# Linear attention beside a Mish feed-forward, one core: two pairs of token tiles turned when only centred, key weights by transposing loads, and a new order

## The chip, the cores and the metric

The kernel runs on one core of a Trainium2 chip. What counts is the device time of one execution in microseconds (us). The kernel before has a median of 154.43 us in three runs (154.17, 154.43 and 155.7).

The names of the engines in this text: PE does matmuls and transposes (PEld is its load of the stationary operand), ACT activations, DVE vector work, POOL vector and mask work, SP only issues DMAs. ACT can issue DMAs too. "SPq" and "ACTq" in the profile are the instruction queues of the two in which DMA issues show.

## The reference

`x` is 2048 tokens by 448 columns in bfloat16. It is normalised over the columns, and the result is x plus two branches of the normalised `xn`:

```python
def _layernorm(x, axis=-1, eps=1e-5):
    m = jnp.mean(x, axis=axis, keepdims=True)
    v = jnp.var(x, axis=axis, keepdims=True)
    return (x - m) / jnp.sqrt(v + eps)
...
qkv = (x @ wqkv).reshape(B, S, 3, H, Dh)           # H = 16, Dh = 28
pq = jnp.einsum("bhsd,hdf->bhsf", q, w_phi)        # pk likewise from k
phi_q = concatenate([_softmax(pq), _softmax(-pq)]) # phi_k likewise
kv = jnp.einsum("bhsf,bhsd->bhfd", phi_k, v)
z  = jnp.einsum("bhsf->bhf", phi_k)
num = jnp.einsum("bhqf,bhfd->bhqd", phi_q, kv)
den = jnp.einsum("bhqf,bhf->bhq", phi_q, z)[..., None] + 1e-6
o = (num / den) @ wo
...
h = x @ w1 + b1                                    # 448 -> 1792
act = h * jnp.tanh(softplus(h))                    # Mish
ffn = act @ w2                                     # 1792 -> 448
...
return x + A(xn) + B(xn)
```

## The kernel before, in words

**Tiles.** The 2048 tokens are 16 tiles (`t`) of 128, taken as 8 pairs (`u`). A row of 448 columns is three chunks of 128 and one of 64; in the turned pair (`xnT`, 7 chunks of 128 by 128) the two 64s of a pair share one chunk. So each product of a pair has an "F" part (three full chunks for each of its two tiles, six matmuls) and an "H" part (one 64-row matmul for each tile, on the two halves of the array). `pair_part` (L414) issues them in either order; whichever comes second is followed by the evacuation of PSUM. PSUM has 8 banks, used in four pairs of banks; `take2` gives the pair that has been idle longest, in program order.

**Stages.** For each pair: statistics (`ln_stats`, L443), 1/std (`ln_rstd`, L461, on ACT by Ln and Exp or on POOL by a power), normalising (`ln_pair`, L475, on DVE, or on POOL after a small `shift` on DVE), and turning (`xT`, L508, on PE with an evacuation, or by a transposing DMA on SP). Meanwhile the weights of keys and queries are folded with `w_phi`: the key weights are loaded as they stand, turned on PE (`w_tr`, L540) and evacuated to `WT`; the query weights are loaded by four transposing DMAs (`load_qT`, L279), of which a last 64 columns are doubled by a DVE copy (`double_qT`, L283, step `qd`). `w_mm` (L563) multiplies both with a block-diagonal `Wbd` (built on POOL from `w_phi` and a mask) into `Wp`. Then for each pair three products: `v_mm` (values, evacuated by ACT or DVE), `k_mm` and `q_mm` (each evacuated by two ACT exponentials, of the product and its negative). `k_norm` sums the exponentials on DVE and divides on POOL (line L625); `kv_mm` sums over all pairs into one matrix, which `kvz` masks and turns by a DMA. `q_turn` (L680) turns the query exponentials by DMA, tile by tile. `nd` (L708) multiplies them with that matrix on PE and divides on DVE, `oT` turns the outcome by DMA.

The feed-forward (`ffn1`, L691) computes 14 blocks of 128 hidden columns for each half `q` of the tokens, with a Mish on ACT as evacuation. `ffn2` (g, L811) and `wo` (L823) add both branches in one PSUM bank for each tile, `finish` adds x on DVE, `store` writes it.

**The order.** There is no planner at run time. The string ORDER (L147) is a list of step names, and each step appends its instructions to the queues of the engines it uses; each engine executes its own queue strictly in this order. So the string sets the order on PE, ACT, DVE, POOL and of the DMAs on SP all at once, and an instruction that waits holds back what stands behind it on its engine. Names to follow: `lx2s` loads x's tiles 4 and 5 by SP (x4: tiles 8 to 11, x6: 12 to 15), `z12` issues twelve dummy matmuls, `st2b` are the statistics of pair 2 with one tile on DVE and one on ACT, `rs2p` 1/std on POOL, `xn2d` normalising on DVE, `xt2b` turning on PE with the evacuation on ACT and DVE, `xt1m` turning by DMA, `wtk0b` turning half of the key weights, `wmk0b` and `wmq0d` the folding, `v2Fd` the F part of pair 2's values with DVE to evacuate, `kn4.1` the normalising of pair 4's negative exponentials, `e6` the turning of tile 6's query exponentials, `f1.2H` the H part of block 2 for the second half. At the start the two loads of x2 and x3 stand first, then the key weights, `phi`, tails and biases, and x1, v's weights, x4, the query weights, all on SP.

Of the kernel before, what the change touches and what calls it, by code (L numbers as in the profile page):

```python
# [12 lines left out]
D = 448  # L13
H = 16
DH = 28
# [152 lines left out]
def _kernel(es, nc, A_x, A_wqkv, A_w_phi, A_wo, B_w1, B_b1, B_w2, out):  # L168
# [28 lines left out]
    Wkv = sb("Wkv", [P, 4, 2 * D], BF16)  # L197
    Wk, Wv = Wkv[:, :, 0:D], Wkv[:, :, D:2 * D]
# [3 lines left out]
    zeros = sb("zeros", [P, 2], BF16)  # L202
# [9 lines left out]
    WT = [Eq0[0:GP, i * 1024:(i + 1) * 1024].rearrange("p (c g n) -> p c g n", c=2, g=G) for i in range(2)]  # L212
# [753 lines left out]
```

## Time and profile before

| | us |
|---|---|
| median of 3 runs | 154.43 |
| lowest, highest | 154.17, 155.7 |
| span of the profiled execution, first to last instruction | 152.5 |
| first dummy matmul | 0.95 |
| first useful PE instruction | 6.70 |
| first product of x (v2) | 9.87 |
| first exponential on ACT | 14.44 |
| first POOL division of k_norm | 27.88 |
| first kv product | 55.40 |
| last matmuls end, end of span | 149.5, 152.5 |

The profile comes from one execution, whose span from its first to its last instruction is 152.5 us; its own device time is not listed apart from the runs', and the median of the runs is 1.9 us above the span. The page of the profile has six parts: busy time of each engine, the span in 40 slices with a digit for tenths of busy time, DMA queues, the chain of work that ended last, the costliest groups of instructions by line, and DMA issues. Further views list an engine's instructions in order of time (start, duration, engine, line, operation, what is written and read, how many in a row, and in brackets the idle time before with its releaser), who waited for whom, and the instructions of one tile. A matmul's record lasts longer than the distance to the next one, since matmuls are pipelined; so distances of starts are what one reads for PE.

### The profile page before, as it was taken

To read this page: it belongs to the slowest core of one execution; us is meant where nothing else is said; L and a number is where in the kernel's file an instruction comes from. 1 tells how busy PE (TensorE), PEld (TensorE's weight loads), DVE (VectorE), ACT (ScalarE), POOL (GpSimd) and SP (SyncE) were. 2 spreads that over 40 slices of the span, in tenths; PEclk is the share of its full clock that TensorE was granted. 3 is DMA by queue.
4 is the path that set the end of the run, shared out by engine and by line. 5 is a ranking of instruction groups with operands and counts; after the bars stand their busy time and mean duration, and the time that the engine had idled before them with its cause. 6 is when DMAs were issued, how large, how long until landed. Compare 5 with 4: busy or idle time off the path is not lost.

```text
span 152.5 us, 2888 instructions
## 1 busy us (share of the span) xinstructions
PE 147.9 (97%) x1181; PEld 72.7 (48%) x1181; DVE 101.2 (66%) x227; ACT 74.9 (49%) x91; POOL 39.9 (26%) x58
## 2 busy tenths in 40 slices
PE   7899999999998999999999999999999999999993
PEld 2365444454443466444444444555555555455552
DVE  1699997999999203198999847798695970311221
ACT  4888899898599996757459657100000000000000
POOL 7452552499999950000000000000000000000000
PEclk9999999999999999999999999999999999999999
DMA  5995576889969176830379941030206111110302
GB/s 130 274 238 97 175 136 127 177 236 257 189 141 192 24 160 55 135 71 0 64 149 302 338 75 25 4 62 6 54 0 195 50 34 26 60 34 0 120 0 90
DMA packets 39961, 17.17 MB, mean 113 GB/s; under 512 B 33932, under 2 KB 39180, under 8 KB 39948
## 3 DMA queue, kind: packets, MB, share of 16 engines
q1 hardware_dynamic: 39804, 16.89, 49.2%
q8 instruction: 9, 0.15, 0.4%
q10 hardware_dynamic: 144, 0.10, 0.2%
q14 instruction: 4, 0.03, 0.1%
HBM read 7.02 MB, written 1.84 MB: 58 GB/s over the span
## 4 chain that ended last, share of the span: by engine, by line
PE 82%; DMA 7%; ACT 6%; SPq 2%; DVE 0%; issue 0%; ACTq 0%
PE PS L426 40%; PE PS L816 28%; PE PS L832 7%; DMA EqT<-actT 4%; DMA Wkv<-in_A_wqkv_dram 3%; PE PS L716 3%; PE PS L642 2%; ACT actT L613 2%; ACT actT L693 1%; ACT actT L674 1%; PE PS L575 1%; ACT L693 1%; ACT v_all L504 1%; SPq L268 1%; SPq L682 1%; PE PS L551 0%
## 5 line engine op out<-in xcount | busy, mean ns | idle before, releaser
L426 PE MATMUL PS<-xnT,W 128*128 128x512 bf16 (+1 forms) x224 | 46.3, 379 | 0.0
L816 PE MATMUL PS<-W,actT 128*128 128x448 bf16 (+1 forms) x224 | 42.8, 351 | 0.0
L693 ACT ACTIVATE actT<-PS,b1T 128x1024 bf16<-128x1024 f32 x28 | 30.3, 1114 | 13.1 <-PE PS L426 13.0
L816 PEld LDWEIGHTS PS<-W,actT 128*128 128x128 bf16 x224 | 21.8, 98 | 20.2 <-issue 0.4
L426 PEld LDWEIGHTS PS<-xnT,W 128*128 128x128 bf16 (+1 forms) x224 | 17.6, 97 | 23.7 <-issue 5.1
L625 POOL TENSOR_TENSOR actT<-actT,rSk 128x896 bf16<-128x896 bf16 x16 | 26.6, 1701 | 4.4 <-DVE rSk L623 4.4
L781 DVE TENSOR_TENSOR x_all<-PS,x_all 128x448 bf16<-128x448 f32 (+1 forms) x16 | 9.6, 617 | 20.9 <-PE PS L816 17.7
L621 DVE TENSOR_REDUCE Sk<-actT 128x32 f32<-128x896 bf16 x16 | 16.7, 1042 | 0.9 <-ACT actT L613 0.9
L613 ACT ACTIVATE actT<-PS 128x896 bf16<-128x896 f32 x16 | 13.7, 940 | 0.4 <-PE PS L426 0.4
L426 PE MATMUL PS<-Wpq,xnT 128*128 128x448 bf16 (+1 forms) x64 | 12.9, 353 | 0.5 <-ACT actT L693 0.5
L426 PE MATMUL PS<-Wpk,xnT 128*128 128x448 bf16 (+1 forms) x64 | 12.7, 353 | 0.0
L426 PE MATMUL PS<-Wkv,xnT 128*128 128x448 bf16 (+1 forms) x64 | 12.6, 353 | 0.0
L731 DVE COPY Sq<-PS 128x16 f32<-128x16 f32 x32 | 4.0, 167 | 10.8 <-PE PS L716 10.8
L456 DVE BATCH_NORM_STATS2 stats<-x_all 128x6 f32<-128x448 bf16 x14 | 8.5, 605 | 3.4 <-DMA x_all<-in_A_x_dram 3.4
L739 DVE TENSOR_TENSOR v_all<-v_all 128x464 f32<-128x464 f32 x16 | 10.3, 642 | 0.6
L735 DVE TENSOR_TENSOR v_all<-PS,Sq 128x464 f32<-128x464 f32 x16 | 10.3, 641 | 0.5
L742 DVE TENSOR_TENSOR xn<-v_all,rden 128x448 bf16<-128x448 f32 x16 | 10.0, 625 | 0.6
L737 DVE TENSOR_TENSOR v_all<-PS,Sq 128x464 f32<-128x464 f32 x16 | 10.1, 629 | 0.0
L674 ACT ACTIVATE actT<-PS 128x896 bf16<-128x896 f32 x10 | 8.5, 932 | 1.7 <-DMA EqT<-actT 1.7
L426 PEld LDWEIGHTS PS<-Wpq,xnT 128*128 128x128 bf16 (+1 forms) x64 | 5.3, 97 | 6.5 <-issue 1.1
L426 PEld LDWEIGHTS PS<-Wpk,xnT 128*128 128x128 bf16 (+1 forms) x64 | 5.3, 97 | 6.1 <-issue 1.9
L426 PEld LDWEIGHTS PS<-Wkv,xnT 128*128 128x128 bf16 (+1 forms) x64 | 5.0, 97 | 5.7 <-issue 1.5
(86 smaller groups left out, 118.0 us busy)
## 6 DMA issues: line engine op xcount, KB each, us to landing
W<-in_B_w_dram SPq DMA_DIRECT2D x1, 1568.0 KB, 7.8
out_dram<-x_all SPq DMA_DIRECT2D x7, 224.0 KB, 2.2
W<-in_B_w_dram SPq DMA_DIRECT2D x1, 1344.0 KB, 9.0
x_all<-in_A_x_dram SPq DMA_DIRECT2D x4, 224.0 KB, 3.2
x_all<-in_A_x_dram SPq DMA_DIRECT2D x2, 448.0 KB, 4.6
Wkv<-in_A_wqkv_dram SPq DMA_DIRECT2D x2, 336.0 KB, 4.5
Wo<-in_A_wo_dram SPq DMA_DIRECT2D x2, 336.0 KB, 3.9
W<-in_B_w_dram SPq DMA_DIRECT2D x2, 224.0 KB, 3.6
```

Of the source, the lines that this page charges most:

```text
L426: ins = e.matmul(o, lhs(c, k), rhs(c, k), start=first and c in (0, 3), stop=not first and c in (2, 3))
L613: op("ACT", lambda e, s=s: e.activation(E_of(u)[:, s, :, :], two(b, D), ACT.Exp, scale=1.0 if s == 0 else -1.0), r=[pb(b), pb(b + 1)], w=[ ...
L621: op("DVE", lambda e: e.tensor_reduce(Sk[u][:, s, :], Eh(), AX.X, ALU.add), r=[("E", u, s)], w=[("Sk", u, s)], tag=f"Sk{u}.{s}")
L625: op("POOL", lambda e: e.tensor_tensor(Eh(), Eh(), ap_on(rSk[u][:, s, 0:1], [[1, 2 * H], [0, DH]]), ALU.mult), r=[("E", u, s), ("rSk", u, ...
L674: op("ACT", lambda e, s=s: e.activation(Eq_of(u)[:, :, s, :].rearrange("p i (h n) -> p i h n", n=64)[:, :, :, 0:QP], two(b, D).rearrange(" ...
L693: op("ACT", lambda e: e.activation(actT[:, fc, q * 1024:(q + 1) * 1024], bank(b, 2), ACT.Mish, bias=b1T[:, fc:fc + 1]), r=[("b1T",), pb(b) ...
L735: op("DVE", lambda e: e.tensor_tensor(tv(t1[i]), num(0), sx(1), ALU.mult), r=[pb(b), pb(b + 1), ("Sq", i, 1)], w=[("t1", i)], tag=f"ta{t}")
L737: op("DVE", lambda e: e.tensor_tensor(tv(t2), num(1), sx(0), ALU.mult), r=[pb(b), pb(b + 1), ("Sq", i, 0)], w=[("t2",)], tag=f"tb{t}")
L739: op("DVE", lambda e: e.tensor_tensor(t1[i], t1[i], t2, ALU.add), r=[("t1", i), ("t2",)], w=[("t1", i)], tag=f"tc{t}")
L742: op("DVE", lambda e: e.tensor_tensor(o_sb[(t // 2) % 2][:, t % 2, :].rearrange("p (h d) -> p h d", d=DH), t1[i][:, :, 0:DH], ap_on(rden[i ...
L816: ins = e.matmul(bank(b)[:, 0:width(t)], actT[:, fc, tok(t)], W2[:, fc, 0:width(t)], start=first and fc == 0, stop=last and fc == FC - 1)
L832: ins = e.matmul(bank(b)[:, 0:n], oT_of(u)[lo:hi, cc * P:(cc + 1) * P], Wo[lo:hi, cc, 0:n], start=first and c in (0, 3), stop=last and c i ...
```

## The change

- **Two pairs turned when only centred.** For pairs 1 and 3 (`CEN`) a new step `xc` subtracts the mean on DVE without 1/std; `xtc1a` and `xtc3a` turn this on PE into `cT`, which lies in the still unused block 0 of `actT`, with the evacuation on ACT. The value products of these two pairs read `cT`, and their evacuation multiplies by 1/std, tile by tile. Both pairs are normalised in full too (`xn1p`, `xn3p` on POOL) and turned by DMA (`xt1m`, `xt3m`) for everything else. Pair 2 is turned on PE as before; pair 3 no longer in its normalised form.
- **Key weights by four transposing loads.** `w_tr` goes, with its 16 transposes on PE and their evacuations; `load_T` loads the key weights turned, as it does those of the queries, and `kd` doubles their last 64 columns on DVE. Values keep a main load and two tails.
- **Statistics, 1/std and W1 in finer steps.** `ln_stats` takes one tile; W1 is loaded in three chunks and two tails, with its chunks further apart in the order.
- **Dummies.** `z16` instead of `z12`, on the constant 1.0, without a memset to wait for.
- **Order.** A new ORDER. The first DMAs are on two queues: ACT issues x2, x1, v's tails and phi ahead of its table load, x3 right behind it, x4 behind pair 2's evacuation and x0 behind that of centred pair 1; SP issues the first key load, v's main load, the other three key loads, the four query loads, `xt1m`, x6, `xt3m` and so on. Pairs 0, 1, 3, 4 are normalised on POOL, 2, 5, 6, 7 on DVE. PE begins with the dummies, `xt2b`, `xtc1a`, the values of 2 and 1, `wmk`, pair 3's turn, `k2F`, `wmq`, the values of 3.

```diff
 ORDER = """
...
+lx2a lx1a pi z16 pw pv st5d st4d lvta lpa lkT2s lvms table lkT3s lx3a pm rs2a lkT1s st3d lkT0s st2a xn2d xc1 bd rs1p
+xt2b lqT3s lqT2s lx4a xtc1a v2Fa st7d xn1p kd st6d lqT1s lqT0s xc3 rs3p lx0a v2Ha v1Hd wmk0a wmk1b st8d xt1m v1Fa
+xtc3a xn3p qd st10d st9d k2F st11d wmq1a wmq0a st0d lx6s v3Fd rs5a v3Hd pp rs4p xn4p k2H k1H k1F q1F q2H st1d q1H xt3m
+st12d st14d st15d k3H l1ts k3F q2F xn5d rs7p rs0p q3F st13d xt4m rs6p xt5m v4Fd xn7d l1m0s xn0p pk k4H xn6d v4Hd q3H
+k4F kn3.0 kn1.0 lbs xt7m v5Fd xt6m k5F xt0m k5H v5Hd e4 e5 e7 l1m1s e6 k7H v7Hd k7F v7Fa v0Fd k6F kn4.0 kn2.0 kn2.1 b1
+k6H kn4.1 l1m2s q6H v0Hd kn5.1 e3 k0H k0F e2 q6F q4F q5F q5H e12 e13 e11 f0.3H v6Ha ep kn5.0 kn6.1 q4H kn6.0 v6Fd e9
+f0.3F f1.3F e8 f1.0F f1.3H q7H f1.0H kn7.0 kn0.1 kn0.0 kn3.1 q0H q7F q0F f0.0F f0.2F f1.10F f0.0H f0.2H kn7.1 kv3 kv6
+kv2 l2s kv5 e14 kv0 kv4 los kn1.1 kv7 kv1 kvz e15 e1 f1.1H f0.1H f1.10H f0.1F f0.12F f1.1F f1.12F f1.12H f0.12H f1.9H
...
+wo3H nd12 nd13 g7 g8 wo4F wo3F wo2F g4 nd14 nd15 sto4 ot6m g5 wo6F g6 ot7m g14 g10 g11 g12 wo5H wo6H wo7H wo2H wo7F
+wo5F g13 g15 sto2 sto3 sto6 sto1 sto5 sto0 stt14 stt15
...
+    CEN = (1, 3)
+    cT = {u: actT[:, 0, n * 1024:n * 1024 + 7 * P].rearrange("p (c n) -> p c n", n=P) for n, u in enumerate(CEN)}
...
+    def load_T(name, dst, at, g, eng):
+        dma(eng, lambda e: e.dma_start_transpose(dst[:, g, 0:D], A_wqkv[:, at + g * GP:at + g * GP + P]), w=[(name, g)],
+            tag=f"ld{name}{g}")
...
+    def ln_center(u):
+        X = xn[u % NXN]
+        for t in (2 * u, 2 * u + 1):
+            parts = [(0, D, 0)] if t % 2 == 0 else [(384, D, D), (0, 384, D + 64)]
+            for n, (lo, hi, at) in enumerate(parts):
+                op("DVE", lambda e, t=t, lo=lo, hi=hi, at=at: e.tensor_scalar(
+                    X[:, at:at + hi - lo], x_all[:, t, lo:hi], mv[:, t, 0:1], 0.0, op0=ALU.subtract, op1=ALU.add),
+                   r=[("x", t), ("mean", t)], w=[("xn", u % NXN, t % 2, n)], tag=f"xc{t}.{n}")
...
-    def w_tr(h, eng):
...
     def w_mm(which, h, eng):
         b = take2(False)
         n = GP
 
+        name, T = (("WqT", WqT), ("WkT", WkT))[which]
+
         def lhs(c, g):
-            if which:
-                return WT[h][:, c, g, :]
-            return WqT[0:GP, g, (2 * h + c) * P:(2 * h + c + 1) * P]
+            return T[0:GP, g, (2 * h + c) * P:(2 * h + c + 1) * P]
...
     def v_mm(u, part, eng):
         def then(b):
-            evac(eng, lambda: v_all[:, u, :, :, 0:DH], lambda: two(b, D).rearrange("p i (h d) -> p i h d", d=DH),
-                 [pb(b), pb(b + 1)], [("v", u)], f"ve{u}")
...
+            for i in range(2):
+                t = 2 * u + i
+                dst = v_all[:, u, i, :, 0:DH]
+                src = bank(b + i)[:, 0:D].rearrange("p (h d) -> p h d", d=DH)
+                if eng == "ACT":
+                    fn = lambda e, t=t, dst=dst, src=src: e.activation(dst, src, ACT.Copy, scale=rstd[:, t:t + 1])
+                else:
+                    fn = lambda e, t=t, dst=dst, src=src: e.tensor_scalar(dst, src, rstd[:, t:t + 1], 0.0, op0=ALU.mult,
+                                                                          op1=ALU.add)
+                op(eng, fn, r=[pb(b + i), ("rstd", t)], w=[("v", u, i)], tag=f"ve{t}")
```

207 lines of the change are left out of this document (94 added, 113 removed).

## The prediction

> **What bounds the kernel now.** I read the page first, then the chain of waits, then the waits of PE alone, then the timeline of each engine over the first 60 us.
>
> ```profile
> span 152.5 us, 2888 instructions
> ...
> PE   7899999999998999999999999999999999999993
> ...
> ACT  4888899898599996757459657100000000000000
> ```
>
> Only in the last slice is PE below 7 tenths. ACT is nearly as full up to slice 16; at the end it is free. The page warns that ends of matmuls are modelled, so I look at where matmuls start. The chain of waits gives their pace, and its last pieces give the tail:
>
> ```profile
> 7.97 0.65 PE PS L551 x8
> 8.63 0.40 PE PS L499 x7
> ...
> 9.14 0.89 PE PS L575 x16
> ...
> 139.28 10.23 PE PS L816 x56
> ...
> 149.53 0.56 DVE x_all L781
> ```
>
> Transposes go at 0.40/7 = 0.057 us each, the small weight products (L575) at 0.056, the 448-column matmuls at 10.23/56 = 0.183. After the last matmul 152.5 - 149.5 = 3.0 us are left, the last sum and its store. PE's own waits, and the rows at the start and around its one long gap:
>
> ```profile
> PE PS L551 <- DMA Wkv<-in_A_wqkv_dram: 0.7, 2, 0.4
> PE PS L426 <- ACT actT L693: 0.5, 1, 0.5
> ...
> 0.95 5.30 PE L371 MATMUL PS<-zeros 128*128 128x512 bf16 x12 [0.95 <-POOL zeros L314]
> 6.70 0.63 PE L551 MATMUL PS<-ident,Wkv 128*112 128x128 bf16 x8 [0.45 <-DMA Wkv<-in_A_wqkv_dram]
> 7.18 0.56 PE L499 MATMUL PS<-ident,xn 128*128 128x128 bf16 x7
> ...
> 40.01 6.43 PE L426 MATMUL PS<-xnT,W 64*128 64x512 bf16 x32
> 46.90 0.36 PE L426 MATMUL PS<-Wpq,xnT 64*128 64x448 bf16 x2 [0.46 <-ACT actT L693]
> ```
>
> So this execution is 6.7 us of start, 142.8 us of PE that hardly pauses, 3.0 us of tail. Two places lose time after 6.70. The 15 transposes from 6.70 need 15 x 0.057 = 0.86 and would be through at 7.56, but the next start at 7.97: 0.41 lost on the key weights' landing. And the last of the 32 starts at 40.01 + 6.43 - 0.38 = 46.06, the next could follow some 0.3 later, and starts at 46.90: about 0.55 lost on ACT. About 1.0 us can be won there; beyond this only fewer PE steps or an earlier start can help. ACT, DVE and POOL count only where PE waits for them.
>
> **The change part by part, PE's work.** Sixteen transposes of the key weights go (2 x 8, 16 x 0.057 = -0.91); seven of pair 3 come, since pairs 1, 2, 3 instead of 2 and 3 are turned on PE (+0.40). All other products are the same in number and size. The order changes how often PE goes between full-height steps and half-height ones (the 64-row "H" parts, and nd):
>
> ```profile
> 24.50 0.35 PE L426 MATMUL PS<-Wpq,xnT 64*128 64x448 bf16 x2
> 24.69 0.35 PE L426 MATMUL PS<-Wpk,xnT 64*128 64x448 bf16 x2
> 24.97 1.31 PE L426 MATMUL PS<-Wkv,xnT 128*128 128x448 bf16 x6
> ```
>
> Two H parts are 0.19 apart, an H part and the full one behind it 0.28: a change of height costs 0.09. Counted in the two orders, these changes go from 42 to 44: +0.19. Sum of PE's work: -0.91 + 0.40 + 0.19 = **-0.3**.
>
> **The start.** Sixteen dummies instead of twelve, on a constant, so from about 0.75. At 5.30/12 = 0.44 each they end at 7.8. But PE goes at full pace from 6.70 on (the transposes at 0.057), while the dummies go at half of it (512 columns in 0.44, against 448 in 0.183 later). If the turn comes as early as 6.7 again, 13 are done by then and three go at about 0.22: 7.3. I take 7.3, bounds 7.0 and 7.8. Their input is ready before:
>
> ```profile
> 0.80 0.86 SPq L268 DMA_DIRECT2D x_all<-in_A_x_dram  x2
> 0.80 1.28 ACT L308 ACT_TABLE_LOAD   x1 [0.80 <-PEq L951]
> ...
> 3.39 0.63 DVE L456 BATCH_NORM_STATS2 stats<-x_all 128x6 f32<-128x448 bf16 x1 [3.39 <-DMA x_all<-in_A_x_dram]
> 4.05 0.18 DVE L458 BATCH_NORM_AGGREGATE mv<-stats 128x2 f32<-128x6 f32 x1
> ...
> 11.47 0.89 DVE L491 TENSOR_SCALAR xn<-x_all,mv,rstd 128x448 bf16<-128x448 bf16 x3
> ...
> 7.92 0.48 ACT L504 ACTIVATE xnT<-PS 128x384 bf16<-128x384 bf16 x1
> ...
> 9.16 0.91 ACT L504 ACTIVATE xnT<-PS 128x896 bf16<-128x896 bf16 x1
> ```
>
> x2 is still the first load, now from ACT's queue, so the statistics begin near 3.4, and three tiles take 3 x 0.78: 5.7. ACT issues five DMAs (0.43 each as SP's two, tails and phi somewhat more: 3.4), then the table load (4.7), then one more (5.1), then two small steps for 1/std, about 0.5 together: 5.7. xn2 ends at 6.7, the centring of pair 1 at 7.7. The start is thus **+0.6** against 6.70, set by the dummies and not by data. Then pair 2 is turned, evacuated (0.48 on ACT, DVE beside it) and v2 begins at 8.3; pair 1 is turned beside that. A gap of about **+0.1** is left; 0 to 0.5 are its bounds.
>
> The Trainium skill ("TensorE: Matmul & The Clock Gate", Part 1) says that the array runs at half its clock until a window of about 3.4 us of sustained work has passed, and that this window runs free of the kernel's start. The half pace of the twelve dummies agrees; when it ends was seen here in one execution only. By that rule the dummies would end anywhere from 6.0 to 7.7 (an estimate), and the sum would move by -0.5 to +0.4.
>
> **The first weights.** The key weights now come by four transposing loads on SP, the query ones behind them; most of x and v's tails go out on ACT. The tile view of WqT has, for its four loads,
>
> ```profile
> DMA to landing us min/median/max: 3.0/3.8/4.8
> ```
>
> and of x:
>
> ```profile
> DMA to landing us min/median/max: 2.6/3.8/4.8
> ```
>
> From the timelines of SP, DVE and POOL:
>
> ```profile
> 5.49 0.49 SPq L268 DMA_DIRECT2D x_all<-in_A_x_dram  x1
> 6.02 5.11 SPq L280 DMA_TRANSPOSE WqT<-in_A_wqkv_dram  x4
> ...
> 13.85 0.23 DVE L284 COPY WqT<-WqT 128x256 bf16<-128x256 bf16 x1
> ...
> 15.47 1.14 DVE L506 CAST Wpq<-PS 128x448 bf16<-128x448 f32 x2
> ...
> 17.50 0.15 DVE L479 SCALAR_TENSOR_TENSOR shift<-mv,rstd 128x2 f32<-128x2 f32 x1
> ...
> 17.76 1.74 POOL L486 TENSOR_SCALAR xn<-x_all,rstd,shift 128x448 bf16<-128x448 bf16 x3 [1.11 <-DVE shift L479]
> ```
>
> At 1.28 an issue and 0.43 for v's main load, the fourth key load is issued at 5.1 and lands at 8.1 to 9.9. Its copy (kd) stands on DVE behind tile 7's statistics and pair 1's shift, done at 9.5; PE, after v2 (1.3) and v1's H part, which waits for pair 1's evacuation (ACT, 9.6), gets there at 9.85. No wait; 0.7 if it lands at its latest. PE then has wmk (0.9), v1F (1.1), pair 3's turn (0.4) and k2F (1.1): 13.5. Now it wants the query weights, whose copy (qd) is behind st8 on DVE, and st8 waits for x4, which is issued on ACT's queue behind pair 2's evacuation, at 8.2 instead of 5.49. It lands 3.8 to 4.8 later (median and far end of x's row; it is one of the two large ones): 12.0 to 13.0. st8 0.8, shift 0.15, qd 0.23: 13.2 to 14.2. PE waits **+0.3** (bounds 0 and 0.7). Queued behind qd are st10, st9, st11, st0 (0.78 each), v3's evacuation (2 x 0.6, as the CASTs above) and pair 4's shift.
>
> **Pair 4.** Its xn moves from DVE (0.89) to POOL (1.74). From qd at 13.9: four statistics and v3's evacuation end at 18.2, POOL at 20.0, its transposing load lands 3.0 later at 23.0. PE by then has done wmq and v3 (13.8 + 0.9 + 1.3 = 16.0), and of k2, k1, q1, k3, q2, q3 five F parts, five H parts and some changes of height (5.6 + 1.0 + 0.3): 22.9. **+0.2**, bounds 0 and 0.7.
>
> **ACT, and the old gaps.** ACT gets one turn more (0.91) and the other half of the query weights (about as much), and loses two key evacuations, one tile's statistics and two v evacuations, each of them of the size of these rows or less; so it has no more to do in all. But its first exponentials come behind the evacuations of v2, wmk, v1, pair 3 and wmq, at about 16.9 instead of 14.44 (first row below): from 10.0 on 0.9, 1.5, 1.1, 0.9, 2.0 and 0.5 for pair 5's 1/std. I let the old losses go (**-1.0**) and put **+0.4** for PE waiting on PSUM that ACT has not read, with bounds of 0 and 1.1, twice the 0.55 measured now.
>
> ```profile
> 14.44 1.73 ACT L613 ACTIVATE actT<-PS 128x896 bf16<-128x896 f32 x2
> ...
> 30.32 24.89 POOL L625 TENSOR_TENSOR actT<-actT,rSk 128x896 bf16<-128x896 bf16 x15 [0.74 <-DVE rSk L623]
> ...
> 55.40 3.33 PE L642 MATMUL PS<-actT,v_all 128*60 128x112 bf16 x128
> ```
>
> POOL does three xn more (5.2), all before 26, in time that it idles now; phi then starts near 27.5 and needs 16 x 1.66 = 26.6: 54.1. PE reaches the first kv near 53.5 and the last at 56.4. Cost nothing; if that cover goes, each microsecond of POOL is one of PE.
>
> **Tail.** Same last token, same 3.0. Four stores are now queued behind token 13's sum on SP: **+0.1**, bounds 0 and 0.5.
>
> **Sum.** +0.6 - 0.3 + 0.1 + 0.3 + 0.2 - 1.0 + 0.4 + 0.1 = +0.4 on a span of 152.5. The runs' median, 154.43, stands 1.9 above that span; I add to it: **154.8 us**. With all bounds low the sum is -1.0, with all high +4.0.
>
> **The rivals.**
> A, DVE's queue becomes the bound: x4, 448 KB, shares the DMA engines with the four query loads (112 KB each). Their bytes begin to move near 9.9; 0.9 MB from there, at the 150 to 280 GB/s of these slices
>
> ```profile
> GB/s 130 274 238 97 175 136 127 177 236 257 189 141 192 24 160 55 135 71 0 64 149 302 338 75 25 4 62 6 54 0 195 50 34 26 60 34 0 120 0 90
> ```
>
> take 3.2 to 6 us: landing 13.1 to 15.9, and PE waits 0.8 to 3.5 at qd; all of DVE's later work shifts with it. With the middle (landing 14.5, wait 2.2 instead of 0.3) the time is 156.7. It decides, by 1%, from a landing at about 13.8 on. For it: st8 heads a strict queue. Against: x's row has 4.8 at most, and much was in flight then too. The Trainium skill ("DMA: Bandwidth & Descriptors", "Issuing engines are not separate DMA queues") has the loads of both issuers share the same 16 engines; no run here shows it for ACT and SP together.
> B, no new wait: dummies end at 7.0, the gaps at qd, pair 4 and PSUM are nil: +0.3 - 0.3 - 1.0 + 0.1 = -0.9, 153.5. For it: each of these waits is a few tenths between bounds that include nil. Against: four must be nil together.
> C, the middle: ACT's later start or POOL's phi holds kv back by 1.5 us: 155.9 to 156.3. For it: ACT's slices of 7 to 9 tenths up to slice 16. Against: ACT has less to do in all.
> D, it does nothing: normalising was never what PE waited for, so centred pairs gain nothing, and the order's small changes cancel: 154.4.
>
> **How the numbers follow.** My forecast 0.40 (153.9 to 155.6), D 0.15, A 0.18, C 0.12, B 0.15. About 1% (1.5 us) is what a measurement of this kernel can tell from no change: 152.9 and 156.0 are the borders. B falls below the lower one with an earlier start too, 0.08, and 0.02 come from the edges of the others: faster 0.10. Most of A (0.16), half of C (0.06) and a tenth of my own (0.04): slower 0.26. Same 0.64. Range: the low end takes B with 0.6 to spare (152.9), the high end takes A's middle (156.9).
>
> **What would show it.** First transposes of xn (L499's step) at 7.0 to 7.8; v2's first matmul near 8.3; the query weights' product (L575's second group) near 14.0, with the copy WqT as its releaser and st8 waiting for x_all on DVE; the first kv product at 53 to 55 (now 55.40); the last matmul near 149.9. I am wrong if PE waits over 1 us in one place before 25 us, if ACT's first exponentials come after 18, or if POOL's phi starts after 29.

## The result and the profile after

The changed kernel takes 155.94 us (median of 14 runs, 155.22 to 156.64), the kernel before on the same chip 154.57 (14 runs, 153.7 to 155.7). The ratio is 1.0082, 95% interval 1.0062 to 1.0102: the change costs 1.4 us, slower by 0.8%, which is inside the 1% that the forecast took as no change. The profiled execution of the changed kernel took 155.95 us, with a span of 153.9 against 152.5 before. 1.4 more in the span is the whole difference, so what follows is read from these two spans. Some executions of the variants below lose a few us to a reduced granted clock of PE; the ratios leave out those more than 1.5% above the fastest of their kernel, and the profiled executions of runs 2, 7 and 10 are of this kind (0.989, 0.979 and 0.989 in the mean), so that only their front is read.

The page of the changed kernel, its first line and the slices of PE:

```profile
span 153.9 us, 2901 instructions
...
PE   7779999999999999999999999999999999999992
```

PE is as full as before, from slice 3 to the last but one. No slice shows where 1.4 us went; such small losses only show in the waits of PE and in the distances of its starts. PE's waits by releaser (total, how many, the longest):

```profile
...
PE PS L563 <- DVE WkT L289: 0.8, 1, 0.8
PE PS L563 <- DVE WqT L289: 0.4, 1, 0.4
PE PS L428 <- issue: 0.3, 1, 0.3
```

The wait for pair 2's `xn` before the first turning is left out here. In the changed kernel L507 is the turning of x, L563 the folding of key or query weights, L289 the doubling copy `kd` or `qd`, L428 the products. The old wait for the landing of the key weights is gone; two waits for the doubled weights and one for nothing that the profile names have come. The same places in PE's timeline:

```profile
0.85 4.93 PE L374 MATMUL PS<-const-bfloat16-1.0 128*128 128x512 bf16 x16 [0.85 <-PEq L961]
6.74 1.19 PE L507 MATMUL PS<-ident,xn 128*128 128x128 bf16 x14 [0.96 <-DVE xn L490]
7.88 1.60 PE L428 MATMUL PS<-Wv,xnT 128*128 128x448 bf16 x8
9.32 0.35 PE L428 MATMUL PS<-Wv,actT 64*128 64x448 bf16 x2
10.49 0.96 PE L563 MATMUL PS<-Wbd,WkT 112*128 112x112 bf16 x16 [0.81 <-DVE WkT L289]
...
12.81 1.30 PE L428 MATMUL PS<-Wpk,xnT 128*128 128x448 bf16 x6
14.48 0.96 PE L563 MATMUL PS<-Wbd,WqT 112*128 112x112 bf16 x16 [0.37 <-DVE WqT L289]
...
37.83 2.73 PE L428 MATMUL PS<-Wpq,xnT 128*128 128x448 bf16 x14
40.89 0.39 PE L428 MATMUL PS<-xnT,W 64*128 64x512 bf16 x2 [0.33 <-issue]
```

Read by starts: the first transposes come at 6.74, as before (6.70). Their 14 would take 14 x 0.057 = 0.80 and v2 could start at 7.54; it starts at 7.88, 0.35 late. It needs pair 2's evacuation, which ACT and DVE both begin at 7.34 and ACT ends at 7.83 (7.34 + 0.49); pair 1 is turned in this gap. v1's H part starts at 9.32. The key product behind it goes over to full height, which by the prediction's price takes 0.28 from start to start, so it could follow at 9.60; it starts at 10.49: **0.89 lost**. k2F's last matmul starts at 12.81 + 5 x 0.19 = 13.76, the query product, of full height too, could follow 0.19 later, at 13.95, and starts at 14.48: **0.53 lost**. (The expectations of the runs give these two as 0.97 and 0.44, with the two distances exchanged; the sum is the same.) The last H part ahead of the first feed-forward step starts at 40.20, that step could start at 40.39 and starts at 40.89: **0.50 lost**.

The three causes, from the timelines of POOL, DVE and SP:

```profile
7.92 1.08 POOL L545 TENSOR_TENSOR Wbd<-Wraw,mask 112x224 bf16<-112x224 bf16 x2 [4.72 <-DMA Wraw<-in_A_w_phi_dram]
...
9.28 0.71 POOL L465 TENSOR_TENSOR rstd<-lnv,mhalf 128x2 f32<-128x2 f32 x1
...
10.02 0.16 DVE L478 SCALAR_TENSOR_TENSOR shift<-mv,rstd 128x2 f32<-128x2 f32 x1 [0.76 <-POOL rstd L465]
10.21 0.23 DVE L289 COPY WkT<-WkT 128x256 bf16<-128x256 bf16 x1
...
13.87 0.55 DVE L289 COPY WqT<-WqT 128x256 bf16<-128x256 bf16 x1 [0.35 <-DMA WqT<-in_A_wqkv_dram]
...
35.26 0.62 SPq L277 DMA_DIRECT2D W<-in_B_w_dram  x1
```

The key product waits for `kd` at 10.21. `kd` stands on DVE behind pair 1's shift, this waits for POOL's 1/std, and POOL has the block diagonal ahead of it, for which phi landed at 7.9. The query product waits for `qd`, and `qd` for the last of the four query loads; the copy itself then takes 0.55, where `kd`, of the same size, takes 0.23. The feed-forward waits for W1's third row block: the row gives only "issue", but the block was issued as late as 35.26 and the trace has its landing at 40.80. The chain of waits confirms the second of these; up to PE's long stretch it runs through SP's transposing loads one after the other:

```profile
2.71 1.19 SPq L285
...
9.14 1.26 SPq L285
10.44 3.41 DMA WqT<-in_A_wqkv_dram
...
150.43 0.56 DVE x_all L785
```

The end: the last sum starts at 150.43 instead of 149.53, 0.90 later, and behind it come 3.5 us instead of 3.0. From SP's timeline, before and then after, the stores:

```profile
142.62 5.63 SPq L846 DMA_DIRECT2D out_dram<-x_all  x3
...
150.31 0.33 SPq L843 DMA_DIRECT2D out_dram<-x_all  x1
```

```profile
144.56 6.55 SPq L850 DMA_DIRECT2D out_dram<-x_all  x7
151.21 0.39 SPq L847 DMA_DIRECT2D out_dram<-x_all  x1
```

Before, three stores went out between 142.6 and 148.3, and the last had the queue to itself. After, `sto6` waits for token tile 13's sum, and `sto1`, `sto5`, `sto0` and `stt14` stand behind it, so that all of them go out in the last microseconds ahead of the last one.

### The profile page after: what moved, and what is told of

It reads as the page before. It is cut to its first block, busy times and chain, and to the rows that moved or that the text cites. A ratio compares the mean times of both kernels' runs of the same rounds, so it can differ in the third digit from the quotient of the medians.

```text
span 153.9 us, 2901 instructions
## 1 busy us (share of the span) xinstructions
PE 147.5 (96%) x1176; PEld 72.2 (47%) x1176; DVE 102.2 (66%) x229; ACT 72.7 (47%) x86; POOL 45.1 (29%) x66
## 4 chain that ended last, share of the span: by engine, by line
PE 88%; SPq 6%; DMA 2%; DVE 1%; issue 1%
PE PS L428 48%; PE PS L820 27%; PE PS L836 7%; SPq L285 6%; PE PS L719 3%; DMA WqT<-in_A_wqkv_dram 2%; PE PS L645 2%; PE PS L563 1%; DVE WqT L289 0%; SPq L273 0%; DVE x_all L785 0%; DVE x_all L806 0%; PE PS L690 0%
## 5 line engine op out<-in xcount | busy, mean ns | idle before, releaser
L428 PE MATMUL PS<-xnT,W 128*128 128x512 bf16 (+1 forms) x224 | 46.5, 380 | 0.3 <-issue 0.3
L820 PE MATMUL PS<-W,actT 128*128 128x448 bf16 (+1 forms) x224 | 43.5, 351 | 0.0
L428 PEld LDWEIGHTS PS<-xnT,W 128*128 128x128 bf16 (+1 forms) x224 | 17.8, 97 | 24.9 <-issue 6.0
L428 PE MATMUL PS<-Wpk,xnT 128*128 128x448 bf16 (+1 forms) x64 | 12.9, 353 | 0.0
L428 PE MATMUL PS<-Wpq,xnT 128*128 128x448 bf16 (+1 forms) x64 | 12.2, 353 | 0.0
L456 DVE BATCH_NORM_STATS2 stats<-x_all 128x6 f32<-128x448 bf16 x15 | 9.1, 606 | 4.2 <-DMA x_all<-in_A_x_dram 4.2
L428 PE MATMUL PS<-Wv,xnT 128*128 128x448 bf16 (+1 forms) x48 | 9.7, 352 | 0.0
L428 PEld LDWEIGHTS PS<-Wpq,xnT 128*128 128x128 bf16 (+1 forms) x64 | 5.3, 97 | 5.8 <-issue 0.6
L428 PEld LDWEIGHTS PS<-Wpk,xnT 128*128 128x128 bf16 (+1 forms) x64 | 5.0, 97 | 6.4 <-issue 2.8
L485 POOL TENSOR_SCALAR xn<-x_all,rstd,shift 128x448 bf16<-128x448 bf16 (+2 forms) x12 | 7.1, 602 | 2.5 <-DVE shift L478 2.5
```

The lines of the kernel that those rows point to most:

```text
L428: ins = e.matmul(o, lhs(c, k), rhs(c, k), start=first and c in (0, 3), stop=not first and c in (2, 3))
L820: ins = e.matmul(bank(b)[:, 0:width(t)], actT[:, fc, tok(t)], W2[:, fc, 0:width(t)], start=first and fc == 0, stop=last and fc == FC - 1)
```

## The experiments

Theory: the front of the kernel does gain (no wait for the key weights' landing; v2 two microseconds earlier, since the key product now stands behind it), but everything that is won waits again for loads that the new order puts late: phi and `kd`, the query loads at the end of eight transposing issues on SP, W1's third block; and the order of the stores adds 0.5 at the end. Rivals: that one of the waits alone is the loss and PE keeps what is won there; that the two parts of the change themselves cost the time.

**1. Stores in the order of their sums.**

```diff
-wo5F g13 g15 sto2 sto3 sto6 sto1 sto5 sto0 stt14 stt15
+wo5F g13 g15 sto0 sto1 sto2 sto3 sto5 sto6 stt14 stt15
```

> The changed kernel with one edit: the last stores in the order in which their sums are done (0, 1, 2, 3, 5, 6), so that stores 1, 5 and 0 no longer stand on SP behind token 13's sum. In the changed kernel the last store lands 2.26 us after its issue, before the change 1.72. Theory (a backlog of stores): the landing goes back to about 1.7 and the time falls by 0.5 us, 155.94 to about 155.4. Rival (the tail is what a last store costs after this order of products): no change, within 0.15 us.

Measured: 155.47 (12 runs, 154.74 to 156.65), ratio 1.0049 (1.0018 to 1.0081), span 153.3. From the timeline of its last microseconds:

```profile
148.78 0.81 SPq L850 DMA_DIRECT2D out_dram<-x_all  x2
...
150.41 0.56 DVE L785 TENSOR_TENSOR x_all<-PS,x_all 128x384 bf16<-128x384 f32 x1 [1.65 <-PE PS L820]
...
151.18 0.33 SPq L847 DMA_DIRECT2D out_dram<-x_all  x1
```

The last sum starts as in the changed kernel (150.41 against 150.43), and the span ends 2.9 behind it instead of 3.5. Only two stores are left ahead of the last. The 0.5 at the end is the order of the stores, as the theory had it; the two ratios' intervals overlap, and the tail in the trace decides.

**2. `kd` ahead of pair 1's shift.**

```diff
-xt2b lqT3s lqT2s lx4a xtc1a v2Fa st7d xn1p kd st6d lqT1s lqT0s xc3 rs3p lx0a v2Ha v1Hd wmk0a wmk1b st8d xt1m v1Fa
+xt2b lqT3s lqT2s lx4a xtc1a v2Fa st7d kd xn1p st6d lqT1s lqT0s xc3 rs3p lx0a v2Ha v1Hd wmk0a wmk1b st8d xt1m v1Fa
```

> The changed kernel with one edit: the copy of the key weights (kd) stands on DVE ahead of pair 1's shift, which waits for POOL's 1/std at 9.99, which in turn is queued behind the block-diagonal weights and so behind phi's load. Both theories: the key weights' product starts near 9.75 instead of 10.49. Theory (SP's chain of eight transposing loads is the limit there): the query weights' product still starts at 14.4 to 14.5, since the last query load lands at 13.85, and the time is unchanged within 0.2 us. Rival (the wait for the key weights is a cost by itself): the time falls by 0.7 us to about 155.2.

Measured: ratio 1.0115 (1.0058 to 1.0173). DVE's copy and PE:

```profile
9.53 0.23 DVE L289 COPY WkT<-WkT 128x256 bf16<-128x256 bf16 x1 [0.34 <-DMA WkT<-in_A_wqkv_dram]
...
15.04 0.86 DVE L289 COPY WqT<-WqT 128x256 bf16<-128x256 bf16 x1 [1.80 <-DMA WqT<-in_A_wqkv_dram]
```

```profile
9.81 0.96 PE L563 MATMUL PS<-Wbd,WkT 112*128 112x112 bf16 x16 [0.23 <-DVE WkT L289]
...
15.96 0.96 PE L563 MATMUL PS<-Wbd,WqT 112*128 112x112 bf16 x16 [2.45 <-DVE stats L456]
16.76 2.58 PE L428 MATMUL PS<-Wv,actT 128*128 128x448 bf16 x8
```

With the shift behind it `kd` waits for its own load alone and the key product starts at 9.81 instead of 10.49: 0.68 of its wait was the shift in DVE's queue, and the rest is the load's landing and the copy. But the time is not better. The query product waits for the query loads as before, here even longer, since the last landed at 15.0 instead of 13.85 though it was issued at the same time; whether the edit makes it later is not shown. So the rival that PE keeps the 0.7 falls: its 155.2 lies below the interval of the ratio. In this execution the wait taken away at the key weights came back, and more, at the query weights.

**3. W1's last two row blocks earlier.** `l1m1s` and `l1m2s` both behind `e4`, ahead of three turnings (`e5`, `e7`, `e6`).

```diff
-k4F kn3.0 kn1.0 lbs xt7m v5Fd xt6m k5F xt0m k5H v5Hd e4 e5 e7 l1m1s e6 k7H v7Hd k7F v7Fa v0Fd k6F kn4.0 kn2.0 kn2.1 b1
-k6H kn4.1 l1m2s q6H v0Hd kn5.1 e3 k0H k0F e2 q6F q4F q5F q5H e12 e13 e11 f0.3H v6Ha ep kn5.0 kn6.1 q4H kn6.0 v6Fd e9
+k4F kn3.0 kn1.0 lbs xt7m v5Fd xt6m k5F xt0m k5H v5Hd e4 l1m1s l1m2s e5 e7 e6 k7H v7Hd k7F v7Fa v0Fd k6F kn4.0 kn2.0 kn2.1 b1
+k6H kn4.1 q6H v0Hd kn5.1 e3 k0H k0F e2 q6F q4F q5F q5H e12 e13 e11 f0.3H v6Ha ep kn5.0 kn6.1 q4H kn6.0 v6Fd e9
```

> The changed kernel with one edit: the second and third chunk of W1 are issued on SP behind the turning of tile 4 and ahead of that of tiles 5, 7 and 6; before, the third chunk was issued at 35.26 and landed at 40.80, and the first feed-forward step of PE, which needs all of W1, started at 40.89 after 0.5 us lost. Theory (W1's last chunk is what PE waits for): PE goes on near 40.4, the time falls by 0.4 to 0.5 us to about 155.5. Rival (PE would wait there for a bank that ACT has not read, or gives it back at the next exponentials because the three turnings come 1.2 us later): the gap moves to 43 to 47 us and the time is unchanged or 0.3 us longer.

Measured: 156.88, ratio 1.0129 (1.0082 to 1.0176), span 154.7. PE and ACT around 40 us:

```profile
40.27 0.38 PE L428 MATMUL PS<-xnT,W 64*128 64x512 bf16 x2
41.73 0.36 PE L428 MATMUL PS<-Wv,xnT 64*128 64x448 bf16 x2 [1.08 <-ACT Eq L677]
```

```profile
39.95 1.73 ACT L677 ACTIVATE Eq<-PS 128x896 bf16<-128x896 f32 x2 [1.39 <-DMA EqT<-Eq]
```

The feed-forward step comes at 40.27 without a wait, and behind it PE loses more than a microsecond for ACT, which waits 1.39 for the turning of an exponential tile whose buffer it wants. SP was full there; what is put ahead delays the turnings. The rival is right in kind, the gain is given back, but earlier than it said (41.7 and not 43 to 47).

**4. All of these, and v's main load on ACT's queue instead of SP's.** The edits of 1 to 3, and `lvma` for `lvms`.

> The changed kernel with all three edits, and v's main load issued on ACT's queue behind phi instead of SP's, which takes 0.6 us off SP's chain ahead of the last query load. Theory (these late loads and the store backlog are what the change lost): 0.5 for the stores, 0.5 for W1, and 0.7 to 1.1 at the two weight products, together 1.7 to 2.1, time about 154.0. Rival (early time is given back later, at ACT's exponentials around 40 to 48 us): 0.5 to 0.8 in all, time about 155.3.

Measured: 156.95, ratio 1.0140 (1.0086 to 1.0195), span 154.7. PE waits 1.0 at v2, since v's main load, now behind phi on ACT's queue, lands at 9.0 instead of 7.0, and 1.1 for ACT at 42 as in the third run. The last query load is issued 0.6 earlier on SP, as intended, but lands at 14.25, later than the 13.85 of the changed kernel: a shorter row on the queue did not bring the data earlier. The theory, 154.0, is wrong by 3 us, and the rival's 155.3 is too low as well: two of the four edits brought waits of their own.

**5. The second part undone: the key weights loaded as they stand and turned on PE.** `load_T` for the keys and `kd` go; a main load and two tails of the key weights on SP and `w_tr` with its 16 transposes come back.

```diff
-lx2a lx1a pi z16 pw pv st5d st4d lvta lpa lkT2s lvms table lkT3s lx3a pm rs2a lkT1s st3d lkT0s st2a xn2d xc1 bd rs1p
-xt2b lqT3s lqT2s lx4a xtc1a v2Fa st7d xn1p kd st6d lqT1s lqT0s xc3 rs3p lx0a v2Ha v1Hd wmk0a wmk1b st8d xt1m v1Fa
+lx2a lx1a pi z16 pw pv st5d st4d lvta lpa lkms lvms table lkts lx3a pm rs2a st3d st2a xn2d xc1 bd rs1p
+xt2b lqT3s lqT2s lx4a xtc1a wtk0b v2Fa st7d wtk1b xn1p st6d lqT1s lqT0s xc3 rs3p lx0a v2Ha v1Hd wmk0a wmk1b st8d xt1m v1Fa
...
```

> The changed kernel with its second part undone: the key weights come by one main load and two tails on SP and are turned on PE (16 transposes, half evacuated on ACT, half on DVE), kd goes; all else in the new order. SP is rid of four transposing loads of 1.28 us and gets about 1.7 us of plain ones. Theory (SP's row of eight transposing loads holds back the query weights, and kd behind the shift holds back the key product): the last query load lands near 10.5 to 11 instead of 13.85, the wait of 0.44 before the query product goes, that of 0.97 before the key product shrinks to 0.3 or less, PE does 0.9 more: together -0.2 us, within 0.5 of it either way. Rival (the transposing loads save PE's 0.9 and cost nothing else): +0.9 us, 156.8.

Measured: 156.69, ratio 1.0153 (1.0123 to 1.0182), span 154.9. DVE and PE at the start:

```profile
4.26 0.63 DVE L459 BATCH_NORM_STATS2 stats<-x_all 128x6 f32<-128x448 bf16 x1 [4.26 <-DMA x_all<-in_A_x_dram]
```

```profile
7.44 1.19 PE L510 MATMUL PS<-ident,xn 128*128 128x128 bf16 x14 [0.58 <-DVE xn L493]
...
15.08 0.96 PE L584 MATMUL PS<-Wbd,WqT 112*128 112x112 bf16 x16
```

The query product no longer waits for its loads, since SP has four long issues fewer ahead of them, and the key product doesn't wait either (11.46, 0.29 behind the H part ahead of it). But x2, issued on ACT's queue as before, lands at 4.26 instead of 3.56 now that SP issues plain loads beside it, everything at the start is 0.7 later, and PE has its 16 transposes again. So the rival's number came by another sum than its own, and the transposing loads save time in this order: 0.7 us by the medians, 1.1 by the ratios, whose intervals are apart (1.0123 to 1.0182 against 1.0062 to 1.0102).

**6. The first part undone: all pairs normalised before they are turned.** `CEN = ()`, and the first three lines of the order take `rs1a xn1d` and `xn3d` in place of `xc1 rs1p xn1p` and `xc3`; the turns of pairs 1 and 3 stand later.

> The changed kernel with its first part undone: pairs 1 and 3 are normalised in full on DVE (1/std of pair 1 on ACT, of pair 3 on POOL) and turned once, on PE; two xn on POOL and two transposing DMAs go. Pair 1's turn stands behind v2's F part, pair 3's behind the query product, and k1's F part ahead of v3. Theory (PE's first 14 us hang on the weights, not on normalising): the key product starts at 10.5 as now and the time stays within 0.4 us of 155.94, or falls a little since SP is rid of two transposing DMAs. Rival (centring lets PE start pair 1 and pair 3 earlier): pair 1's turn 1.3 us later and pair 3's 2 us later cost PE 1 to 2 us, about 157.3.

Measured: 160.52 in the median of all six, ratio 1.0362 (1.0308 to 1.0416), span 157.3. DVE and PE:

```profile
7.99 1.28 DVE L490 TENSOR_SCALAR xn<-x_all,mv,rstd 128x448 bf16<-128x448 bf16 x3 [1.27 <-ACT rstd L471]
```

```profile
9.70 1.29 PE L428 MATMUL PS<-Wv,xnT 128*128 128x448 bf16 x6 [2.36 <-issue]
```

This run has a fault of its own: pair 1's normalising stands on DVE ahead of pair 2's evacuation and waits for ACT's 1/std, so pair 2's values wait 2.4 for something that they don't need. It shows what a strict queue costs, and not what centring is worth, so it decides neither for the theory nor for the rival; the eleventh run does.

**7. Both parts undone, with the stores of the first run.** The edits of 5, 6 and 1.

> The changed kernel with both parts undone (keys turned on PE, no centring), and the stores at the end in the order of their sums; what stays of the change are the new order, the loads split over ACT and SP, finer statistics and W1, sixteen dummies. Theory (both parts by themselves are worth nothing here, the stores cost 0.5): about 155.2, 0.2 to 0.5 above the time before the change, since the new order still waits at W1's third chunk. Rival (the two parts carry a gain that late loads hide): 156.5 or more.

Measured: 160.93 in the median of all six, ratio 1.0391 (1.0352 to 1.0430). It has the fault of the sixth run too, so no more is read from it than this: this order with the old means is far from the kernel before. How much of that is the fault, and how much the order, it doesn't show.

**8. Twelve dummies instead of sixteen.** `z12` for `z16`.

> The changed kernel with twelve dummies instead of sixteen. In the changed kernel's profile the sixteen end at 5.8 and PE then waits 0.96 us for pair 2's normalised tiles. Theory (the start is set by x2's landing, its statistics and xn2, not by the dummies): the first transposes stay at 6.7 and the time within 0.3 us of 155.94. Rival (the forecast's: the dummies set the start): 0.4 to 0.9 us earlier, 155.3. A third case: PE idles longer and its clock falls back to half, +0.5 to +1.5 us.

Measured: 156.2, ratio 1.0121 (1.0083 to 1.0159). PE's start:

```profile
0.85 4.34 PE L374 MATMUL PS<-const-bfloat16-1.0 128*128 128x512 bf16 x12 [0.85 <-PEq L961]
6.81 1.19 PE L507 MATMUL PS<-ident,xn 128*128 128x128 bf16 x14 [1.62 <-DVE xn L490]
```

With four dummies fewer the transposes start at the same time, 6.81 against 6.74: they wait for pair 2's `xn` and not for the dummies, whose number is worth nothing here. The theory holds.

**9. The stores of run 1, and W1's blocks in an idle stretch of SP.** The two blocks leave their places further down the order and go right behind W1's tail, near 18 us.

```diff
-st12d st14d st15d k3H l1ts k3F q2F xn5d rs7p rs0p q3F st13d xt4m rs6p xt5m v4Fd xn7d l1m0s xn0p pk k4H xn6d v4Hd q3H
+st12d st14d st15d k3H l1ts l1m1s l1m2s k3F q2F xn5d rs7p rs0p q3F st13d xt4m rs6p xt5m v4Fd xn7d l1m0s xn0p pk k4H xn6d v4Hd q3H
...
```

> The changed kernel with its stores in the order in which their sums come, and with the second and third row block of W1 issued on SP right behind W1's tail (near 18 to 20 us, where SP stands idle) instead of at 33.4 and 35.3 us, in the middle of the row of turning transfers. Theory, that the third block's lateness (0.5 us of PE at 40.2) and the order of the stores (0.5 us at the end) are two plain losses: no wait for W1 on PE, and both are won, 1.0 below the changed kernel, so 154.9 or a ratio of 1.002 to the kernel before. Unlike the earlier try, nothing is put ahead of a turning transfer that is due, and from 33 us on SP has 1.2 us less to issue, so turnings may come earlier. Rival, that PE's gain at 40 us is given back within the next microseconds because ACT's exponentials or the turned tiles are what is due there: only the stores are won, 155.4, ratio 1.005, with a new wait of 0.3 to 0.6 on PE between 40 and 48 us.

Measured: ratio 1.0119 (1.0082 to 1.0156). The profiled execution took 156.05. PE near 25 us:

```profile
24.99 1.30 PE L428 MATMUL PS<-Wv,xnT 128*128 128x448 bf16 x6 [1.22 <-DMA xnT<-xn]
```

The wait for W1 at 40 is gone, and another of 1.22 has come at pair 4's values, which the changed kernel started at 23.65 with no wait. Pair 4's turning was issued at 20.29 (20.45 in the changed kernel) and landed at 24.9. The rates of the DMA engines, of the changed kernel and of this one, 3.85 us a slice, show what it met:

```profile
GB/s 137 227 298 135 182 165 183 194 195 243 215 192 173 342 285 80 190 42 0 128 4 0 60 64 45 16 64 0 60 0 4 91 28 0 60 4 0 79 82 256
```

```profile
GB/s 140 237 244 191 181 295 289 218 191 169 2 168 180 298 285 114 195 75 0 110 22 0 60 64 11 51 64 0 60 0 0 63 60 0 112 71 0 25 154 119
```

In the sixth and seventh slice (19.3 to 27 us) 295 and 289 GB/s instead of 165 and 183. SP was idle there, the engines behind it were not. Neither theory nor rival had this: both looked at SP's queue, and the collision is in the transfers. The Trainium skill ("DMA: Bandwidth & Descriptors", "Issuing engines are not separate DMA queues") says that all transfers interleave on the same 16 engines whoever issues them; the landing at 4.6 us behind the issue, where the changed kernel had 2.9, agrees. Here SP issues both, so the two-queue side of that statement is not tested by this run.

**10. The same, with phi as the second load of ACT's queue.**

```diff
-lx2a lx1a pi z16 pw pv st5d st4d lvta lpa lkT2s lvms table lkT3s lx3a pm rs2a lkT1s st3d lkT0s st2a xn2d xc1 bd rs1p
+lx2a lpa lx1a pi z16 pw pv st5d st4d lvta lkT2s lvms table lkT3s lx3a pm rs2a lkT1s st3d lkT0s st2a xn2d xc1 bd rs1p
```

> The same, with the load of w_phi issued as the second on ACT's queue (1.2 us) instead of the fifth (3.0 us); x1's tiles and v's tail are issued 0.4 later. Theory, that the key weights' product waited for phi by way of POOL's block diagonal, POOL's 1/std, pair 1's shift and the doubling of the key weights behind it on DVE: phi lands near 6, the key product starts at 9.7 to 10.0 instead of 10.5 and PE's wait there falls to 0.2 to 0.5. The query product still waits for the last of SP's eight transposing issues, near 14.4, so the time won is lost again there: within 0.3 of the run without this edit. Rival, that what PE gets ahead at the key product it keeps: 0.5 below the run without this edit.

Measured: ratio 1.0228 (1.0173 to 1.0282). From POOL's, DVE's and PE's timelines:

```profile
4.50 1.08 POOL L545 TENSOR_TENSOR Wbd<-Wraw,mask 112x224 bf16<-112x224 bf16 x2 [1.29 <-DMA Wraw<-in_A_w_phi_dram]
```

```profile
6.62 0.63 DVE L456 BATCH_NORM_STATS2 stats<-x_all 128x6 f32<-128x448 bf16 x1 [1.49 <-DMA x_all<-in_A_x_dram]
...
10.08 0.23 DVE L289 COPY WkT<-WkT 128x256 bf16<-128x256 bf16 x1
```

```profile
8.30 1.19 PE L507 MATMUL PS<-ident,xn 128*128 128x128 bf16 x14 [2.40 <-DVE xn L490]
...
27.16 1.98 PE L428 MATMUL PS<-Wv,xnT 128*128 128x448 bf16 x6 [3.13 <-DMA xnT<-xn]
```

The block diagonal comes 3.4 earlier, and x1, issued 0.5 later than in the changed kernel, lands so late that its statistics start 1.6 later (6.62 after a wait for it, instead of 5.05 without one). Pair 1's statistics stand on DVE ahead of pair 2's `xn`, so the start is 1.6 later, and `kd` is no earlier than before (10.08). Whether phi alone, landing earlier, would have freed the key product stays open: this run doesn't show it.

**11. Centring undone once more, without the sixth run's fault.**

```diff
-    CEN = (1, 3)
+    CEN = ()
...
-lx2a lx1a pi z16 pw pv st5d st4d lvta lpa lkT2s lvms table lkT3s lx3a pm rs2a lkT1s st3d lkT0s st2a xn2d xc1 bd rs1p
-xt2b lqT3s lqT2s lx4a xtc1a v2Fa st7d xn1p kd st6d lqT1s lqT0s xc3 rs3p lx0a v2Ha v1Hd wmk0a wmk1b st8d xt1m v1Fa
+lx2a lx1a pi z16 pw pv st5d st4d lvta lpa lkT2s lvms table lkT3s lx3a pm rs2a lkT1s st3d lkT0s st2a xn2d bd
+xt2b lqT3s lqT2s rs1a xn1d lx4a v2Fa xt1a v2Ha kd st7d st6d lqT1s lqT0s rs3p lx0a v1Hd wmk0a wmk1b xn3d st8d v1Fa
...
```

In the third line `xt3a` stands in place of `xtc3a xn3p`, and `xt3m` goes.

> The changed kernel with its first part undone a second time: all pairs are normalised before they are turned, and this time pair 1's normalisation stands on DVE behind pair 2's evacuation and its 1/std on ACT behind pair 2's evacuation, so that pair 2's values no longer wait for it. Theory, that centring is worth the stretch from pair 1's statistics to its 1/std and back, and saves DVE two slow passes: pair 2's values at 7.9 as in the changed kernel, pair 1's turn near 10.0 and not 9.2 or earlier, a new PE wait of 0.7 to 1.5 there, and pair 3's turn later too: 157, ratio 1.016. Rival, that centring as such is worth nothing and the 4.6 us of the first try were the queue on DVE alone: 156, the changed kernel's own time, ratio 1.008.

Measured: 157.18, ratio 1.0162 (1.0131 to 1.0193), span 155.2. PE:

```profile
8.02 1.31 PE L428 MATMUL PS<-Wv,xnT 128*128 128x448 bf16 x6 [0.58 <-ACT xnT L512]
9.74 0.56 PE L507 MATMUL PS<-ident,xn 128*128 128x128 bf16 x7 [0.41 <-DVE xn L490]
...
11.32 0.36 PE L428 MATMUL PS<-Wv,xnT 64*128 64x448 bf16 x2 [0.71 <-ACT xnT L512]
11.61 0.96 PE L563 MATMUL PS<-Wbd,WkT 112*128 112x112 bf16 x16
```

v2 at 8.02 as in the changed kernel, pair 1's turn at 9.74, a wait of 0.71 for its evacuation, and the key product at 11.61 instead of 10.49. The delay stays: the query product, now without a wait, starts at 15.70 instead of 14.48. 157 was the theory's number. Centring is worth 1.2 us in this order (157.18 against 155.94, and 0.008 between the ratios), where the rival gave it nothing.

No run beats the kernel before; the best is the first, at 1.0049. The two parts put into the old order were not tried.

## Why the forecast was right, point by point

154.8 was forecast and 155.94 measured: inside the range (152.9 to 156.9), in the class "within 1%", and 1.1 us too low. The class held, but not the likeliest case as it was drawn: its band ends at 155.6, and the time lies in that of rival C (155.9 to 156.3), whose mechanism didn't come. Part of this is luck, since errors on both sides nearly cancel and the border of the class, 156.0, is close. Of the signs set beforehand, the first kv product and the copy `WqT` as the releaser came as said; the first transposes (6.74) and v2 (7.88) were earlier, and PE's long stretch ended at 150.4 instead of 149.9. The terms, measured by distances of starts in the two profiled executions:

| term | forecast | measured |
|---|---|---|
| start | +0.6 | 0.0 (6.74 against 6.70) |
| PE's work | -0.3 | -0.7 (what is left) |
| gap around the first turns | +0.1 | +0.35 |
| key product | 0 | +0.89 |
| query product | +0.3 | +0.53 |
| pair 4 | +0.2 | 0 |
| old losses | -1.0 | -1.0 |
| PSUM and ACT | +0.4 | +0.3 |
| W1's third block | not seen | +0.50 |
| tail | +0.1 | +0.5 |
| sum | +0.4 | +1.4 |

The old losses are both gone and stand at the prediction's price. "PSUM and ACT" are two gaps of 0.2 and 0.1, at 47.55 and 52.8. The work is not measured by itself: it is what is left of the last sum's delay (0.90) when the other terms ahead of it are taken out, so it holds every small gap too, and why it is 0.4 below the forecast stays open.

- **Start.** The step "the start is thus +0.6, set by the dummies and not by data" fails in the changed kernel's execution. Its dummies start 0.43 apart up to 3.36 and 0.22 apart from 3.65 on, so PE was at full pace there and not only from 6.7; sixteen dummies ended at 5.8 and `xn` decided. Run 8 shows it: four fewer change nothing. This end also lies ahead of the prediction's other estimate, 6.0 to 7.7. But the step is not wrong everywhere: where full pace comes late, the sixteen dummies do set the start. In run 9 their row lasts to 7.20 and the first transposes come at 7.03, without a wait, and in run 11 to 7.05 and 6.89. So the term of 0.0 is partly the luck of this execution.
- **Gap around the first turns.** From the first transposes to v2 the forecast had 1.0 us (7.3 to 8.3), the run 1.14 (6.74 to 7.88). The mechanism is as forecast: v2 waits for pair 2's evacuation, which takes the 0.49 that was put for it.
- **Key product.** "No wait; 0.7 if it lands at its latest." The landing was right (9.46, in the forecast's 8.1 to 9.9). What failed is the time of the shift ahead of `kd`, put at 9.5: it came at 10.02, since POOL's 1/std stood behind a block diagonal that waited for phi. The forecast followed DVE's queue and SP's, and not POOL's. This is the largest error, and run 2 shows the shift's part in it: 0.68 of the 0.89.
- **Query product.** The size was nearly right, the cause was not. x4, which rival A was built on, landed at 11.2 and held nobody up; `qd` waited for the last query load, at the end of SP's row of eight issues of 1.25 us. Some 0.3 of the 0.53 is the copy itself, which took 0.55 where the forecast had 0.23. So rival A's place was right and its transfer wrong.
- **Pair 4, POOL, kv.** v4 starts at 23.65 without a wait and kv at 54.76, in the forecast 53 to 55; rival C didn't come. POOL's phi starts at 28.66 and ACT's first exponentials at 17.26, each a little later than forecast and inside what was set as the limits.
- **W1.** The prediction had no term for the loads of W1, though the order moves its blocks between the turnings on SP: a step that is moved, and not counted. In runs 3 and 9 the wait for W1 goes when these loads are moved, but each time another wait of 1.1 or 1.2 takes its place.
- **Tail.** "Four stores are now queued behind token 13's sum on SP: +0.1, bounds 0 and 0.5" had the mechanism, and the size is the upper bound. Run 1 shows it.
- **Rival D**, that normalising was never what PE waited for, falls by run 11; rival B, no new wait, by the table.

So where did the gain go? Against the same order without them, centring is worth 1.2 us (run 11) and the transposing key loads about 1 (run 5). If the two add up, the rest of the change costs some 3.5; that they add up is not shown, since the run without both, the seventh, has a fault of its own. Where the new order waits is read from the trace: `kd` behind a shift that phi holds back, the query weights behind eight long issues on SP, W1's last block in the fullest stretch of that queue, the stores in an order other than that of their sums. Only for the last is a gain shown by mending it (0.5). The waits are coupled: in run 2 one reappears at the next weights, in runs 3, 4 and 9 they change place, so what the others cost by themselves stays open.

## What to carry to other kernels

When a copy or product is moved, follow every queue that its operands pass, the one of the engine that makes a small factor (here POOL's 1/std) too; and price a row of DMA issues by its length on the issuing queue as well as by the transfers, since the last one's landing is what the consumer waits for; run 4 shortened the row and the landing was no earlier. A load that is moved to an idle place of its queue still meets the transfers in flight: look at the rates of the DMA engines in that stretch first. Issue stores in the order in which their sums come.

## What the runs showed of the hardware

- **When PE gets its full pace varies between executions.** Sixteen dummies took 4.93 us in the changed kernel, 6.01 in run 5 and 6.35 in run 9; twelve took 4.34 in run 8, where twelve had taken 5.30 before. The Trainium skill ("TensorE: Matmul & The Clock Gate", Part 1) says that the window that decides runs free of the kernel's start; these numbers agree.
- **A long wait of PE can cost twice.** Behind the wait of 2.45 in run 2 the products go at half pace (eight in 2.58 instead of 1.60), behind that of 3.13 in run 10 six in 1.98 instead of 1.30; behind 2.36 in run 6 they go on at full pace (six in 1.29). Each is one execution. The Trainium skill ("TensorE: Matmul & The Clock Gate", Part 1) says that an idle window of some 3.4 us brings the half clock; here a wait of 2.45 was enough, so the measurement differs.
- **A transposing load holds SP for 1.2 to 1.3 us** (the rows at L285), a plain one for 0.4 to 0.6. Eight of them are 10 us of that queue.
- **The same DVE copy took 0.55 and 0.86 us** (`qd`, in the changed kernel and in run 2) instead of 0.23 (`kd`). In both, POOL was at work when the copy began; in run 4 it was too, and the copy took 0.23. The cause was not tested.
